# Two row sums ahead of the M sums, one load from another queue, and M_A's blocks in other banks: a gated mix of two linear-attention blocks

## The chip, the core and the metric

One Trainium2 chip; the program runs on one of its cores. The metric is the device time of one execution in microseconds. A run consists of several executions of the changed kernel and of the kernel before on the same chip, and medians are compared. Profiles come from single executions taken with the hardware profiler. In them PE is TensorE (matrix products), PEld its weight loads, DVE is VectorE, ACT ScalarE, POOL GpSimd and SP SyncE; "SPq" and "ACTq" are the instructions with which SyncE and ScalarE start DMA transfers.

## What is computed

The input `x` has 2048 rows of 640 in bf16. Two linear-attention blocks A and B with weights of their own work on the same `x`, and a gate mixes them. Cut to what matters:

```python
g = sigmoid((x * gate_w).sum(-1, keepdims=True))
# for A and for B, with H = 32 heads of Dh = 20:
q, k, v = split(x @ wqkv)
pq, pk = phi(q), phi(k)               # phi(t) = where(t > 0, t + 1, exp(t)) + 1e-6
kv  = einsum("bhsd,bhse->bhde", pk, v)
z   = einsum("bhsd->bhd", pk)
num = einsum("bhqd,bhde->bhqe", pq, kv)
den = einsum("bhqd,bhd->bhq", pq, z)[..., None] + 1e-6
block = (num / den) @ wo
out = g * block_A + (1 - g) * block_B
```

## The kernel before

**The algebra.** The kernel never forms v. For each block it computes G, the product of `x` with `pk` (640 x 640), then kv of each head as the masked blocks of the product of `wv` with G, then M, the product of kv with `wo` (640 x 640). The denominators and the gate go as factors into the rows of `pq` (`scale`, line 760). Then `out` is one product, the row pair of both scaled `pq` times M_A over M_B.

**The stages.** First the k and q products of A with phi behind them (`k_chunk`, `q_block`, `q_strassen`), then G of A, then k and q of B, from about 71 us to 114 us in the profile, in a stage whose PSUM pool is called "weave"; then a stage "after" with G of B, and the M of A in between; then the M of B, and then the output. Many of the products are written as Strassen-Winograd schemes with 7 products for 8, so VectorE makes sums and differences of operands.

**PSUM.** [...] `ps(name, slot)` gives a tile of two banks in one of four numbered slots, a `cell` one bank. "weave" allocates slots 3 and 2 and then four cells `q0` to `q3`, which `q_strassen` calls ce, cf, co and cz. When it closes, slot 2 of the next stage gets a pool of its own ("hold2", on the right side of PSUM, line 1059), and "after" allocates the others on the left as they are first used. A new tile waits for the last users of the tiles whose banks it takes over.

**M_A.** `g_pass` (line 477) makes the last 128 rows of B's G: 16 row blocks of `x`, two products each. In the middle of it, behind 16 of the 32 products, it calls `between` (line 1061), and there the first three of six blocks of M_A are made. `m_a(g, slot)` (line 667) is two products of [120, 120] by [120, 320] into the slot's two banks, a copy by ScalarE to SBUF, and a store of these 120 rows to `m_rows` in DRAM by SyncE (`m_store`, line 664). Blocks 3 and 4 come behind `g_pass` (lines 1062, 1063), block 5 inside `g_strassen` (line 551), always in slot 2. M_A is then read back from DRAM in another layout (row = 5 x partition + index).

**M_B.** Its six blocks (`m_b`, line 675) are made between 139 and 143 us, copied by ScalarE and VectorE half each, and stored by SyncE. Then `m_load` reads M_B back in three loads of two blocks each (rows 0 to 239, 240 to 479, 480 to 639; lines 1097 and 1098). A load waits for the stores of its own rows.

**The output.** The rows of `out` are taken in 8 pairs: pair i is rows 128 i and 1024 + 128 i. With the lower and upper halves of both `pq` as a 2 x 2 block matrix and the column halves of M_A and M_B as another, seven products p1 to p7 of five matmuls each make the four quarters of a pair (class `Pair`, line 784):

- p1 is lower `pq_A` by M_A's left half and p2 lower `pq_B` by M_B's left half; both into bank `w`, which gives quarter c11
- p5 is upper `pq_A` by TM0, into bank `z`
- p6 is the row sum s2 by TM1, on top of p1 in bank `x`; ScalarE copies the result to `u2` (line 837)
- p7 is a row difference (D3) by TM2, into bank `y`; VectorE adds `u2` and gives `u3` (lines 841, 779)
- c22 is the addition of p5 and `u3`; p4, upper `pq_B` by TM3, goes on into bank `y` and p3, the row sum s4 by M_B's right half, on into bank `z`

There are two banks of each kind, for even and odd pairs, so p4 of a pair may begin only when `u3` has read bank `y`.

The operands' sums are VectorE's:

- `p_sums(rows, ks)` (line 722), on 256 rows at a time (two pairs): k=1 adds `pq_B` upper to `pq_A` upper in place, k=2 makes s2 in the lower rows of `xT`, k=4 makes s4 in its upper rows. One is 128 x 1280 elements. `part[0]` serves pairs 0 and 1, `part[1]` pairs 2 and 3, and so on
- `m_sum(k)` (line 733): TM2, TM1 and TM3 from M_B, M_A and TM0, in this order, 128 x 1600 elements each

**The order.** It is written out by hand (lines 1087 to 1148) under a manual schedule: each engine does its instructions in the order in which the program names them, and semaphores are set by the dependences. Around the change it is: blocks 2 to 5 of M_B, with p1 of pair 4 in between; the copy of that p1 to SBUF (`p1_out`, line 1096); the three loads; the scaling of B's last rows (line 1099); `p_sums` with k=1 for parts 0 and 1, k=2 and 4 for part 0; p1 of pairs 5, 6, 7, 2 and 3, then of 0; p5 of pairs 2 and 3; p1 of pair 1; p5 of pairs 0 and 1; the three M sums; `p_sums` with k=2 and 4 for part 1; p2 and c11 of pairs 0 and 1; p7, p6 and c22 of both; p4 and p3 of pair 0; then a loop over pairs 1 to 7.

Of the kernel before, what the change touches and what calls it, by code (L numbers as in the profile page):

```python
# [17 lines left out]
DT = D // P  # L18
# [6 lines left out]
NG = 6  # L25
# [8 lines left out]
def kernel(  # L34
# [11 lines left out]
    nc = tc.nc  # L46
# [12 lines left out]
    def new_stage(name):  # L59

        if stage:
            stage.pop().close()
        if name is not None:
            held = ctx.enter_context(ExitStack())
            stage.append(held)
            pools["ps"] = held.enter_context(late_pool(name))
# [20 lines left out]
    def ps(name, slot=None):  # L87

        return banks(ps_raw(name, slot))
# [387 lines left out]
    def g_pass(b, c, slot, between=None, at=ST // 2):  # L477

        pt = ps(f"g{'AB'[b]}", slot)
        for i in range(ST):  # L480
            if between is not None and i == at:
                between()
            for hf in range(2):
                g_mm(c, i, hf, pt)
        for hf in range(2):
            nc.scalar.copy(out=GT[hf][:, c, :], in_=pt[:, hf, 0:HF])

    def g_mm(c, i, hf, pt):
        nc.tensor.matmul(  # L489
            pt[:, hf, 0:HF], lhsT=xn[:, i, c * P:(c + 1) * P], rhs=pk[:, i, hf * HF:(hf + 1) * HF],  # L490
            start=(i == 0), stop=(i == ST - 1),
        )
# [159 lines left out]
    def m_block(b, g, banks, to=None):  # L652

        at = f_rows[g].start
        for hf in range(2):
            nc.tensor.matmul(
                banks[hf][:K6, 0:HF], lhsT=kv6[b][:K6, at:at + K6], rhs=wo_sb[b][:K6, g, hf * HF:(hf + 1) * HF],
                start=True, stop=True,
            )
        if to is None:  # L660
            to = work.tile([P, D], BF16, tag="osb", name="m5", bufs=3)
        return to[:f_rows[g].stop - at]

    def m_store(g, to):
        nc.sync.dma_start(out=m_rows[f_rows[g], :], in_=to)

    def m_a(g, slot):

        pt = ps("mA", slot)
        to = m_block(0, g, cells(pt), M[0][:, g, :] if g < DT else None)  # L670
        n = to.shape[0]
        nc.scalar.copy(out=to.rearrange("p (b n) -> p b n", b=2), in_=pt[:n, :, 0:HF])
        m_store(g, to)

    def m_b(g, banks):

        to = m_block(1, g, banks, held["mb"][:, g, :] if g < DT else None)
        n = to.shape[0]
        for hf, copy in enumerate((nc.scalar.copy, nc.scalar.copy if g < 2 else nc.vector.tensor_copy)):
            copy(out=to[:, hf * HF:(hf + 1) * HF], in_=banks[hf][:n, 0:HF])  # L680
        m_store(g, to)

    def m_load(g0, g1):

        rows = slice(f_rows[g0].start, f_rows[g1 - 1].stop)
        nc.sync.dma_start(
            out=M[1][rows.start // DT:rows.stop // DT], in_=m_rows[rows, :].rearrange("(p m) d -> p m d", m=DT)
        )

    def cells(pt):  # L690
        return [pt[:, hf] for hf in range(2)]
# [22 lines left out]
    def add_rows(dst, a, b, op):  # L714
        nc.vector.tensor_tensor(out=dst, in0=a, in1=b, op=op)  # L715
# [6 lines left out]
    def p_sums(rows, ks=(1, 2, 4)):  # L722

        up = slice(SH + rows.start, SH + rows.stop)
        a11, a21, a12, a22 = [pqT[b][:, :, r] for b in range(2) for r in (rows, up)]
        s2, s4 = xT[:, :, rows], xT[:, :, up]
        for k, dst, a, b, op in (
            (1, a21, a21, a22, ALU.add), (2, s2, a21, a11, ALU.subtract), (4, s4, a12, s2, ALU.subtract)
        ):
            if k in ks:  # L730
                add_rows(dst, a, b, op)

    def m_sum(k):

        lo, hi = slice(0, HF), slice(HF, D)
        a, b = M[0], M[1]
        if k == 1:
            add_rows(TM[1][:], b[:, :, hi], TM[0][:], ALU.subtract)
        elif k == 2:
            add_rows(TM[2][:], b[:, :, hi], a[:, :, hi], ALU.subtract)  # L740
        else:
            add_rows(TM[3][:], b[:, :, lo], TM[1][:], ALU.subtract)
# [17 lines left out]
    def scale(b, m):  # L760

        rec = R[:].rearrange("p h j n -> p (h j n)")
        nc.vector.tensor_tensor(out=pqT[b][:, m, :], in0=pqT[b][:, m, :], in1=rec, op=ALU.mult)
# [187 lines left out]
    def bank(pool, name, n=1):  # L951
        return pool.tile([P, HB] if n == 1 else [P, n, HB], FP32, tag=name, name=name)

    with tc.manual_schedule():
# [103 lines left out]
        hold = ExitStack()  # L1058
        pools[2] = hold.enter_context(tc.tile_pool(name="hold2", bufs=1, space=bass.MemoryType.PSUM, reuse_waits="tile", side="right"))
        new_stage("after")  # L1060
        g_pass(1, DT - 1, 0, lambda: [m_a(g, slot) for g, slot in enumerate((2, 1, 3))])
        m_a(3, 2)
        m_a(4, 3)
        part = [slice(n * RB, (n + 1) * RB) for n in range(4)]
        held["mb"] = wpool.tile([P, DT, D], BF16, tag="wk", name="MBr")

# [26 lines left out]
        pairs[4].p1(None, (2, 3, 4))  # L1093
        m_b(4, acc["z"])
        m_b(5, acc["w"])
        pairs[4].p1_out()
        for g in range(0, NG, 2):
            m_load(g, g + 2)
        scale(1, 4)
        for rows, ks in ((0, (1,)), (1, (1,)), (0, (2, 4))):  # L1100
            p_sums(part[rows], ks)
# [10 lines left out]
        inner = ctx.enter_context(late_pool("inner"))  # L1112
        acc["y"] = [bank(inner, f"oy{n}") for n in range(2)]
        TM[3] = wpool.tile([P, DT, HF], BF16, tag="wk", name="TM3")
        for k in (2, 1, 3):
            m_sum(k)
        p_sums(part[1], (2, 4))
        for p in pairs[0:2]:
            p.p2()
            p.c11()  # L1120
# [58 lines left out]
```

## Time and profile before

| | us |
|---|---|
| median of 3 runs | 186.67 |
| lowest and highest run | 186.53, 186.91 |
| the profiled execution | 186.59 |
| its span | 184.9 |
| TensorE busy | 179.8 |
| VectorE busy | 148.4 |
| ScalarE busy | 108.5 |

The span runs from the first to the last event of the profiled execution on the core; the device time holds 1.7 us around it. The granted clock of TensorE was 1.0. A row of the timeline gives the start in us, the length in us (of the whole group where it ends in x and a count), the engine, the line of the kernel, the instruction, its output and inputs, and in brackets how long the engine had been idle before it and what released it. [...] In the program's names `xT`, `pqTA`, `pqTB`, `MA`, `MB`, `TM` and `SQ` are SBUF tiles (D3 lies in `SQ`), `ox`, `oy`, `oz`, `ow` the output banks.

### The profile page before, as it was taken

What the parts mean: (1) busy time and instruction counts of PE and PEld (TensorE: products, weight loads), DVE (VectorE), ACT (ScalarE), POOL (GpSimd) and SP (SyncE); (2) the same over time, 40 slices, a digit from 0 to 9 for tenths busy, and PEclk for the clock granted to TensorE, in tenths of its full rate; (3) what the DMA queues carried; (4) which work ended last, traced back from release to release, by engine and by line L of the source; (5) the groups of instructions that cost most, each with busy time, mean ns of one, the idle gap of its engine ahead of it and who ended that gap; (6) DMA issues with size and microseconds to landing.
All of it is one profiled execution on the core that took longest, in us unless ns stands there. A gap on an engine that the chain in (4) does not pass through costs nothing. (4 is left out here: it accounts for less than half of the span.)

```text
span 184.9 us, 3524 instructions
## 1 busy us (share of the span) xinstructions
PE 179.8 (97%) x1357; PEld 120.8 (65%) x1357; DVE 148.4 (80%) x263; ACT 108.5 (59%) x207; POOL 9.1 (5%) x25
## 2 busy tenths in 40 slices
PE   8999999999999999999999999999999998999993
PEld 3666657665667677676666656767678765777772
DVE  0478989999899799898989897969795959678854
ACT  2065489977883553766777778764715745453210
POOL 8920000000000000000000000000000000000000
PEclk9999999999999999999999999999999999999999
DMA  5995559975018000006000000133912830322132
GB/s 181 298 172 78 108 97 330 331 142 177 0 50 230 17 4 0 0 0 181 2 0 0 4 0 2 51 117 117 253 23 63 217 80 0 128 85 76 71 139 74
DMA packets 20848, 18.00 MB, mean 97 GB/s; under 512 B 9120, under 2 KB 20576, under 8 KB 20832
## 3 DMA queue, kind: packets, MB, share of 16 engines
q1 hardware_dynamic: 19968, 16.97, 34.4%
q10 hardware_dynamic: 864, 0.82, 1.3%
q8 instruction: 10, 0.16, 0.4%
q14 instruction: 6, 0.05, 0.1%
HBM read 11.54 MB, written 4.28 MB: 86 GB/s over the span
## 5 line engine op out<-in xcount | busy, mean ns | idle before, releaser
L299 PEld LDWEIGHTS <-xT 128*128 128x128 bf16 x320 | 31.0, 97 | 15.3 <-issue 0.4
L276 DVE TENSOR_SCALAR e<-e 128x640 bf16<-128x640 bf16 (+2 forms) x58 | 19.7, 341 | 6.3 <-ACT e L268 5.9
L299 PE MATMUL kB<-wkB,xT 128*128 128x320 bf16 x160 | 24.2, 299 | 0.0
L299 PE MATMUL kA<-wkA,xT 128*128 128x320 bf16 (+1 forms) x160 | 23.3, 299 | 0.2 <-DMA wkA<-in_A_wqkv_dram 0.2
L268 ACT ACTIVATE e<-q 128x512 bf16<-128x512 f32 x26 | 15.7, 603 | 5.3 <-PE q L417 4.3
L268 ACT ACTIVATE e<-kA 128x640 bf16<-128x640 f32 x16 | 11.3, 713 | 7.7 <-PE kA L299 7.6
L268 ACT ACTIVATE e<-kB 128x640 bf16<-128x640 f32 x16 | 11.4, 710 | 7.6 <-PE kB L299 7.5
L519 PEld LDWEIGHTS <-xn 128*128 128x128 bf16 x128 | 12.3, 98 | 5.4 <-issue 0.6
L352 PE MATMUL qA<-xT,wqA 128*128 128x512 bf16 x60 | 13.4, 379 | 0.0
L352 PEld LDWEIGHTS <-wqA 128*128 128x128 bf16 x64 | 7.5, 118 | 5.9
L287 DVE SCALAR_TENSOR_TENSOR pk<-kB,e 128x640 bf16<-128x640 f32 x12 | 9.9, 822 | 1.0
L837 ACT COPY u<-ox 128x320 f32<-128x320 f32 x8 | 3.4, 426 | 12.4 <-PE ox L774 12.4
L774 PEld LDWEIGHTS <-pqTB 128*128 128x128 bf16 x80 | 7.7, 98 | 4.1 <-issue 1.2
L774 PEld LDWEIGHTS <-xT 128*128 128x128 bf16 x85 | 8.1, 98 | 2.9
L774 PEld LDWEIGHTS <-pqTA 128*128 128x128 bf16 x85 | 8.0, 98 | 2.9
L779 DVE TENSOR_TENSOR osb<-oz,u 128x320 bf16<-128x320 f32 (+1 forms) x18 | 8.0, 453 | 2.3 <-PE oz L774 1.8
L519 PE MATMUL gs<-pk,xn 128*128 128x320 bf16 x64 | 9.4, 299 | 0.0
L287 DVE SCALAR_TENSOR_TENSOR pk<-kA,e 128x640 bf16<-128x640 f32 x10 | 8.2, 820 | 0.9
L435 DVE TENSOR_TENSOR q<-q,p 128x512 f32<-128x512 f32 x12 | 8.3, 692 | 0.8 <-PE q L417 0.6
L268 ACT ACTIVATE e<-qA 128x1024 bf16<-128x1024 f32 x6 | 6.2, 1028 | 4.2 <-PE qA L352 3.9
L489 PEld LDWEIGHTS <-xn 128*128 128x128 bf16 x64 | 6.2, 98 | 3.1 <-issue 0.3
L519 PEld LDWEIGHTS <-S 128*128 128x128 bf16 x64 | 6.0, 98 | 2.6 <-issue 0.5
(193 smaller groups left out, 358.0 us busy)
## 6 DMA issues: line engine op xcount, KB each, us to landing
out_dram<-osb SPq DMA_DIRECT2D x14, 160.0 KB, 1.8
xn<-in_A_x_dram SPq DMA_DIRECT2D x3, 640.0 KB, 5.2
wvA<-in_A_wqkv_dram SPq DMA_DIRECT2D x1, 800.0 KB
wkB<-in_B_wqkv_dram SPq DMA_DIRECT2D x1, 800.0 KB, 4.7
wqB<-in_B_wqkv_dram SPq DMA_DIRECT2D x1, 800.0 KB
wvB<-in_B_wqkv_dram SPq DMA_DIRECT2D x1, 800.0 KB, 4.9
MA<-m_rows SPq DMA_DIRECT2D x1, 800.0 KB
woA<-in_A_wo_dram SPq DMA_DIRECT2D x1, 750.0 KB
```

The lines of the kernel that those rows point to most:

```text
L268: nc.scalar.activation(out=to, in_=part, func=ACT.Exp)
L276: nc.vector.tensor_scalar(self.e, self.e, 1.0, EPS, op0=ALU.min, op1=ALU.add)
L287: nc.vector.scalar_tensor_tensor(out=dst, in0=src, scalar=1.0 + EPS, in1=e, op0=ALU.add, op1=ALU.max)
L299: nc.tensor.matmul(pt[:, hf, 0:n], lhsT=xT[:, c, i * P:(i + 1) * P], rhs=wk[b][:, c, hf * HF:hf * HF + n], start=(c == 0), stop=(c == DT - 1),
L352: nc.tensor.matmul(dst, lhsT=mixed(wq[b][:, c, :], m), rhs=xT[:, c, n * HB:(n + 1) * HB], start=first, stop=last,)
L435: nc.vector.tensor_tensor(out=dst, in0=src, in1=sb, op=ALU.add)
L489: nc.tensor.matmul(pt[:, hf, 0:HF], lhsT=xn[:, i, c * P:(c + 1) * P], rhs=pk[:, i, hf * HF:(hf + 1) * HF], start=(i == 0), stop=(i == ST - 1),
L519: nc.tensor.matmul(pt[:, n, 0:HF], lhsT=left[:, i, n * P:(n + 1) * P], rhs=right[:, i, :], start=(first and i == 0), stop=(i == hc - 1), s ...
L774: nc.tensor.matmul(dst, lhsT=left[:, c, r0:r0 + P], rhs=right[:, c, :], start=(first and c == 0), stop=(c == DT - 1), skip_group_check=not ...
L779: nc.vector.tensor_tensor(out=dst, in0=acc, in1=sb, op=ALU.add)
L837: nc.scalar.copy(out=self.u2[:], in_=self.at("x"))
```

## The change

Four edits in three places:

- `m_load` takes the engine that starts the transfer. The first load, of blocks 0 and 1, is named behind block 5 of M_B and ahead of pair 4's `p1_out`, and ScalarE starts it. The other two stay with SyncE at their place.
- In the stage "after", blocks 0, 1 and 2 of M_A go to slots 1, 3 and 2 (before: 2, 1 and 3).
- Blocks 3 and 4 go to slots 3 and 2 (before: 2 and 3).
- `p_sums(part[1], (2, 4))` stands ahead of the three M sums (before: behind them).

```diff
-    def m_load(g0, g1):
+    def m_load(g0, g1, eng):
 
         rows = slice(f_rows[g0].start, f_rows[g1 - 1].stop)
-        nc.sync.dma_start(
+        eng.dma_start(
             out=M[1][rows.start // DT:rows.stop // DT], in_=m_rows[rows, :].rearrange("(p m) d -> p m d", m=DT)
         )
...
-        g_pass(1, DT - 1, 0, lambda: [m_a(g, slot) for g, slot in enumerate((2, 1, 3))])
-        m_a(3, 2)
-        m_a(4, 3)
+        g_pass(1, DT - 1, 0, lambda: [m_a(g, slot) for g, slot in enumerate((1, 3, 2))])
+        m_a(3, 3)
+        m_a(4, 2)
...
         m_b(5, acc["w"])
+        m_load(0, 2, nc.scalar)
         pairs[4].p1_out()
-        for g in range(0, NG, 2):
-            m_load(g, g + 2)
+        for g in (2, 4):
+            m_load(g, g + 2, nc.sync)
         scale(1, 4)
...
+        p_sums(part[1], (2, 4))
         for k in (2, 1, 3):
             m_sum(k)
-        p_sums(part[1], (2, 4))
         for p in pairs[0:2]:
             p.p2()
```

## The prediction

> **What bounds the kernel now.** I read the page first, then TensorE's waits, the chain of waits, and then the timeline of each engine around the three places that the change touches. The page's first line, and what the waits view answers for TensorE alone from 108 us to the end:
>
> ```profile
> PE 179.8 (97%) x1357; PEld 120.8 (65%) x1357; DVE 148.4 (80%) x263; ACT 108.5 (59%) x207; POOL 9.1 (5%) x25
> PE oy L774 <- DVE u L779: 0.8, 1, 0.8
> ```
>
> TensorE is busy 97% of the span. What can be won without taking work away is therefore its few gaps, and the view names only one for the whole last third: the bank `oy` waited 0.8 us for VectorE's line 779. The chain that ended last, in order of time, shows what stood ahead of that wait:
>
> ```profile
> 153.74 0.74 DVE xT L715
> 154.49 0.02 issue
> 154.51 0.82 DVE xT L715
> ```
>
> Two row sums (`xT`) run right ahead of it. TensorE's timeline at that place (start, length, instruction):
>
> ```profile
> 149.30 1.52 PE L774 MATMUL oz<-TM,pqTA 128*128 128x320 bf16 x10
> 150.78 1.52 PE L774 MATMUL ow<-MB,pqTB 128*128 128x320 bf16 x10
> 152.13 0.84 PE L774 MATMUL oy<-TM,SQ 128*128 128x320 bf16 x5
> 152.81 0.84 PE L774 MATMUL ox<-TM,xT 128*128 128x320 bf16 x5
> 153.49 0.84 PE L774 MATMUL oy<-TM,SQ 128*128 128x320 bf16 x5
> 154.17 0.84 PE L774 MATMUL ox<-TM,xT 128*128 128x320 bf16 x5
> 155.79 0.84 PE L774 MATMUL oy<-TM,pqTB 128*128 128x320 bf16 x5 [0.78 <-DVE u L779]
> ...
> 178.22 0.84 PE L774 MATMUL ox<-TM,xT 128*128 128x320 bf16 x5
> ```
>
> Groups of five products start every 0.68 us (152.13, 152.81, 153.49, 154.17), one product every 0.136. The ten from 149.30, p5 of pairs 0 and 1, would let p2 start at 150.66; it starts at 150.78, **0.12 late**. The five from 154.17, p6 of pair 1, would let p4 of pair 0 start at 154.85; it starts at 155.79, **0.94 late** (the view's 0.78 counts from the modelled end of the last product). From there TensorE sets the pace: the row at 178.22 is 33 groups of five further on, and 22.43 / 33 is 0.68 again. So what is won at 155 us reaches the end in full.
>
> **The row sums.** VectorE's timeline at the same place:
>
> ```profile
> 147.66 0.82 DVE L715 TENSOR_TENSOR xT<-pqTB,xT 128x1280 bf16<-128x1280 bf16 x1
> 150.76 0.99 DVE L715 TENSOR_TENSOR TM<-MB,MA 128x1600 bf16<-128x1600 bf16 x1 [2.27 <-DMA MB<-m_rows]
> 151.67 2.07 DVE L715 TENSOR_TENSOR TM<-MB,TM 128x1600 bf16<-128x1600 bf16 x2
> 153.66 0.82 DVE L715 TENSOR_TENSOR xT<-pqTA 128x1280 bf16<-128x1280 bf16 x1
> 154.51 0.82 DVE L715 TENSOR_TENSOR xT<-pqTB,xT 128x1280 bf16<-128x1280 bf16 x1
> 155.25 0.48 DVE L779 TENSOR_TENSOR u<-oy,u 128x320 f32<-128x320 f32 x1
> ```
>
> Ahead of the first M sum VectorE idles 2.27 us, until B's M has been read back. The two sums that move need 153.66 to 155.33, 1.67 us. Their inputs are ready by then: the k=1 sum of the same rows and the scaling of B's q have run earlier on this engine. Their targets, rows 256 to 511 of `xT` and those 1024 above, are next read for pairs 2 and 3. Put first, they run from 148.50 to 150.17 and end 0.59 before the M sums can begin. They cost nothing; the DMA wait hides them. Only a landing more than 0.59 earlier would take that cover away, and then they would hold up what no product has asked for yet: p7 wants TM2 1.36 after p2 starts.
>
> What is late next at p4? The M sums still end at 153.74. The addition `u` of pair 0 then waits for ScalarE's copy of p6. At the tail the last pair's addition waits for just such a copy, and shows the step between the two engines:
>
> ```profile
> 153.69 0.43 ACT L837 COPY u<-ox 128x320 f32<-128x320 f32 x1 [0.33 <-PE ox L774]
> ```
>
> ```profile
> 179.10 0.43 ACT L837 COPY u<-ox 128x320 f32<-128x320 f32 x1 [2.97 <-PE ox L774]
> ```
>
> ```profile
> 179.56 0.49 DVE L779 TENSOR_TENSOR u<-oy,u 128x320 f32<-128x320 f32 x1 [0.65 <-ACT u L837]
> ```
>
> Start to start that is 0.46, so `u` runs from 154.15 to 154.63. TensorE followed it by 0.06 (155.73 to 155.79), so the bank is free at 154.69; TensorE gets there at 154.85. The slack is 0.16 and the gap closes: **0.94 us**. The addition behind `u` (c22, another 0.5) ends by 155.2, and p3 wants its bank at 155.53.
>
> **M_A's banks.** TensorE around the first M_A blocks, then ScalarE, then VectorE:
>
> ```profile
> 114.68 2.34 PE L489 MATMUL gB<-pk,xn 128*128 128x320 bf16 x16
> 117.08 0.97 PE L656 MATMUL mA<-woA,R 120*120 120x320 bf16 x6
> 117.89 2.34 PE L489 MATMUL gB<-pk,xn 128*128 128x320 bf16 x16
> 120.07 0.71 PE L656 MATMUL mA<-woA,R 120*120 120x320 bf16 x4
> ```
>
> ```profile
> 116.28 0.76 ACT L273 ACTIVATE pqTB<-q,lift 128x512 bf16<-128x512 f32 x1
> 117.55 1.88 ACT L672 CAST MA<-mA 120x640 bf16<-120x640 f32 x3 [0.52 <-PE mA L656]
> ```
>
> ```profile
> 115.81 0.82 DVE L287 SCALAR_TENSOR_TENSOR pk<-kB,e 128x640 bf16<-128x640 f32 x1
> ```
>
> Sixteen products take 2.18 (117.89 to 120.07), so block 0 could start at 116.86. It starts at 117.08, which is 0.04 after ScalarE's activation of `q` ended (117.04). That activation is the last reader of `co` and `cz`, the last two banks that the former stage allocates, and slot 2 belongs to a pool put at the other side of PSUM. With the change block 0 gets slot 1, whose banks were last read by the `kB` chunk (over at 116.63) or, if the layout is another, by something still earlier. Block 0 then starts at 116.86, and block 2, now the one in slot 2, at 117.40, well after 117.04. **0.22 us** come free. What is late next: block 3 needs the copy of block 1, second of the three from 117.55 (0.63 each, so 118.8), block 4 the third (119.43); TensorE comes for them at 120.07. From here to 150 us TensorE's groups and the copies behind them move together. VectorE's sums of k don't, but TensorE's waits view names none that waited for them.
>
> **The first load of B's M.** SyncE's queue, then two rows of the DMA view (the last column is the time from issue to landing), then the issue cost on ScalarE and its timeline:
>
> ```profile
> 141.05 0.98 SPq L665 DMA_DIRECT2D m_rows<-MBr  x2
> 144.77 1.72 SPq L686 DMA_DIRECT2D MB<-m_rows  x3
> 144.77 0.31 SPq L686 DMA_DIRECT2D MB<-m_rows  x1
> ```
>
> ```profile
> m_rows<-MBr SPq DMA_DIRECT2D x5, 150.0 KB, 2.0
> MB<-m_rows SPq DMA_DIRECT2D x1, 200.0 KB, 4.5
> ```
>
> ```profile
> L154 ACTq DMA_DIRECT2D xn<-in_A_x_dram x3: 408/453/454, 0.8 to 2.2; - x3
> 143.62 0.92 ACT L813 COPY GT<-ox 128x320 f32<-128x320 f32 x2
> ```
>
> Load 1 stands at 144.77 behind all six stores on SyncE, though it needs only stores 0 and 1. Store 1 ends its issue at 142.03 and began 0.31 before, at 141.72; 2.0 later, at 143.7, it has landed. ScalarE is through with its copies of M_B at about the same time (the next copy, pair 4's, starts at 143.62), so it hardly waits and issues at about 143.8, 0.97 earlier. Load 3 (the one of 200 KB) goes out at 146.18 (144.77 + 1.72 - 0.31), after the last store's landing, and lands 4.5 later at 150.7. That is the moment that frees VectorE and p2. Is it set by its issue or by the transfers ahead of it? The last two columns here are the share of the DMA engines and GB/s:
>
> ```profile
> 145.50:146.50 1.00, 1.00 (x10) 0.73 (x8) 1.00 (x2) 0.75 (x2) 0.00 (x0) 1.00 0.70 165
> 146.50:149.00 2.50, 2.50 (x20) 1.81 (x19) 1.96 (x3) 1.47 (x5) 0.00 (x0) 1.00 1.04 248
> ```
>
> From 146.5 on they are full, so load 3 waits behind loads 1 and 2; in the microsecond before, 0.30 of their time is free, which an earlier load 1 can fill. So the last landing moves between 0 (the transfers alone decide) and 0.97 (the issue alone decides) earlier, or later if rival 4 holds; I take 0.3, the free share. TensorE can use only the first **0.12** of it, because p5 itself ends at 150.66 behind that.
>
> The cost on ScalarE is one issue of 0.41 to 0.45 and a wait of some 0.1, ahead of pair 4's copy. The banks behind those copies are wanted back late:
>
> ```profile
> 146.58 0.84 PE L774 MATMUL ox<-MA,pqTA 128*128 128x320 bf16 x5
> ```
>
> is p1 of pair 0, which takes pair 4's bank. That copy would now end near 144.7, 1.9 ahead of it, and ScalarE's page share of 59% leaves room to catch up. I cost it at nothing. [...]
>
> [...]
>
> **The sum.** 0.94 + 0.22 + 0.12 - 0.03 = 1.25 us. The profiled execution took 186.59 (its span of 184.9 and 1.7 around it), 0.08 below the median of 186.67 and inside the runs' spread of 186.53 to 186.91. From the median that gives **185.4 us**, 0.7% faster.
>
> **The rivals.**
> 1. The landing doesn't move: the transfers are the limit, as the full engines after 146.5 say, and p2 keeps its 0.12. Then 0.94 + 0.22 = 1.16, so **185.5**. Against it stands the free share before 146.5. [...]
> 2. The bank edit brings nothing, because slot 1 waits as long or slot 2 was not what held block 0. Then 1.03 are left, **185.6**. For it: the waits view names no releaser for these 0.22; I inferred it from two times 0.04 apart. Against it: nothing else ends there.
> 3. Another wait takes p4's place. The slack is 0.16; if `u` of pair 0 came 0.5 later (one more ScalarE copy of 0.43 ahead of it, as ScalarE now has an issue more to do), 0.34 would be lost, **185.75**. Against it: ScalarE waited 0.33 for p6 before that copy.
> 4. Slower: load 1 now shares the engines with stores 2 to 5, and SyncE issues loads 2 and 3 only when these have landed. Each microsecond that the last store lands later goes one to one into load 3, the M sums and p2, and from 1.1 us on it has eaten the rest of the gain. At worst a store beside a load takes as long as a load, 4.5 for 2.0: 2.5 later, less the 1.16, so **188.0**. Against it: the stores of before share the engines among themselves, issued one behind the other, and land in 2.0. For it: they stood ahead of every load in one queue, and now one load is in another.
>
> **How the numbers follow.** Forecast 0.62, rival 1 0.18, rival 2 0.08, rival 3 0.05, rival 4 0.07. A measurement of this kernel can tell about 0.2% (0.37 us) from no change: the runs of before lie 0.14 below to 0.24 above their median. The range takes in the first three cases and rival 3, each with that spread: 185.4 less 0.2 and 185.75 plus 0.2, so 185.2 to 185.95. Of rival 4, 0.03 is a landing late by 0.8 to 1.5, within 0.2%, and 0.04 is later still. So faster 0.93, same 0.03, slower 0.04.
>
> **What would show it.** In the changed kernel VectorE does the two `xT` sums right behind those of part 0, and then still waits some 0.3 us for the load (0.59 less what the landing gains); p4 of pair 0 follows p6 of pair 1 by 0.68, and TensorE's waits view is empty; M_A's block 0 follows the first half of the g pass by 2.18; load 1 stands on ScalarE's queue 0.7 to 1 us ahead of its old place, and p2 follows p5 by 1.36. I am wrong on the load if M lands no earlier, on the banks if block 0 still waits for the end of the activation, and on the whole if p4 keeps a gap or M lands later than 150.7 less 0.22.

## The result and the profile after

| | before | changed |
|---|---|---|
| median of 14 runs each, us | 186.87 | 185.95 |
| lowest and highest, us | 186.44, 187.38 | 185.53, 186.82 |
| profiled execution, us | 186.59 | 186.12 |
| its span, us | 184.9 | 184.4 |

The ratio is 0.9956, with a 95% interval of 0.9943 to 0.9969: 0.44% faster, or 0.82 us of 186.87; the two medians differ by 0.92. The direction was right; forecast were 1.25 us and a range of 185.2 to 185.95, and the median lies at the edge of that. It misses the forecast of 185.4 by 0.55, and 0.20 of this come from the kernel before, which took 186.87 in these 14 runs and 186.67 in the three from which the forecast was counted. The span of the profile fell by only 0.5, because the stage with M_A begins 0.28 us later in it than before, though all the code ahead of it is the same. So the two profiles are compared by distances within a stage.

TensorE around M_A's blocks, and around the output's first pairs, in the changed kernel (start, length):

```profile
114.96 2.34 PE L489 MATMUL gB<-pk,xn 128*128 128x320 bf16 x16
117.13 0.98 PE L656 MATMUL mA<-woA,R 120*120 120x320 bf16 x6
...
149.35 1.52 PE L774 MATMUL oz<-TM,pqTA 128*128 128x320 bf16 x10
151.23 1.52 PE L774 MATMUL ow<-MB,pqTB 128*128 128x320 bf16 x10 [0.36 <-issue]
...
154.63 0.84 PE L774 MATMUL ox<-TM,xT 128*128 128x320 bf16 x5
155.31 0.84 PE L774 MATMUL oy<-TM,pqTB 128*128 128x320 bf16 x5
```

Three distances answer to the three edits. M_A's block 0 follows the g products by 2.17 us (2.40 before): 0.23 won. p4 of pair 0 follows p6 of pair 1 by 0.68 (1.62 before): 0.94 won. But p2 follows p5 by 1.88, where ten products take 1.36 from start to start (1.52 is the row's shown length, 0.16 more): it is 0.52 late, and was 0.12 late before. (The row names no releaser for p2; VectorE's first M sum begins within 0.01 of it, and its row below names the load.) **0.40 us were lost there**, and 0.94 + 0.23 - 0.40 = 0.77 is what the spans show once the later start is taken off (0.5 + 0.28). VectorE at the same place:

```profile
148.46 0.82 DVE L715 TENSOR_TENSOR xT<-pqTA 128x1280 bf16<-128x1280 bf16 x1
149.31 0.82 DVE L715 TENSOR_TENSOR xT<-pqTB,xT 128x1280 bf16<-128x1280 bf16 x1
151.22 0.99 DVE L715 TENSOR_TENSOR TM<-MB,MA 128x1600 bf16<-128x1600 bf16 x1 [1.09 <-DMA MB<-m_rows]
152.13 2.07 DVE L715 TENSOR_TENSOR TM<-MB,TM 128x1600 bf16<-128x1600 bf16 x2
154.61 0.49 DVE L779 TENSOR_TENSOR u<-oy,u 128x320 f32<-128x320 f32 x1 [0.40 <-ACT u L837]
```

The moved row sums ended at 150.13, and VectorE then waited another 1.09 us for the load. So the sums did not push the M sums back; M came late by itself. The loads in the changed kernel: SyncE's queue, what it waited for between 140 and 152 us (in total, times, longest), and ScalarE with its own load. In the queue's rows, one with x2 or x3 spans its whole group, and the row behind it shows the last of the group by itself:

```profile
144.35 0.31 SPq L665 DMA_DIRECT2D m_rows<-m  x1
145.66 3.20 SPq L686 DMA_DIRECT2D MB<-m_rows  x2
148.55 0.31 SPq L686 DMA_DIRECT2D MB<-m_rows  x1
```

```profile
SPq L686 <- DMA m_rows<-m: 1.7, 1, 1.7
SPq L686 <- DMA m_rows<-MBr: 1.6, 2, 0.8
```

```profile
143.90 0.37 ACTq L686 DMA_DIRECT2D MB<-m_rows  x1
144.31 0.76 ACT L813 COPY GT<-ox 128x320 f32<-128x320 f32 x2 [0.54 <-DMA m_rows<-MBr]
144.95 0.44 ACT L813 COPY GT<-mB 128x320 f32<-128x320 f32 x1
```

Load 1 did go out early, at 143.90. Load 3 went out at 148.55, 4.20 behind the last store (144.35), where it was 1.89 before (146.18 and 144.29). The second view says what it stood for last and longest: the landing of that last store, `m_rows<-m`, block 5's 40 rows. Load 3's own time from issue to landing, in the DMA view of the changed kernel, became shorter:

```profile
MB<-m_rows SPq DMA_DIRECT2D x1, 200.0 KB, 2.6
```

2.6 us for 4.5 before, since nothing stood ahead of it any more. The DMA engines show why (last two columns: share, GB/s; first the stretch up to load 3's issue, then the one behind it):

```profile
146.50:148.50 2.00, 2.00 (x17) 1.47 (x15) 1.97 (x4) 1.23 (x4) 0.00 (x0) 1.00 0.80 186
148.50:149.20 0.70, 0.70 (x7) 0.49 (x6) 0.70 (x2) 0.45 (x2) 0.00 (x0) 1.00 0.00 0
149.20:150.40 1.20, 1.20 (x11) 0.88 (x9) 0.90 (x2) 0.51 (x2) 0.00 (x0) 1.00 0.57 171
```

The engines finished loads 1 and 2, whose last packet ended at 148.63. In the 0.7 us of the second row no transfer began, and load 3's first packet came at 149.48. Of the 2.3 us that load 3 went out later, 1.9 came back in its shorter flight, and 0.4 stayed.

### The profile page after: what moved, and what is told of

It is laid out like the page before. It is cut to its first block, busy times and chain, and to the rows that moved or that the text cites. A ratio compares the mean times of both kernels' runs of the same rounds, so it can differ in the third digit from the quotient of the medians.

```text
span 184.4 us, 3525 instructions
## 1 busy us (share of the span) xinstructions
PE 180.2 (98%) x1357; PEld 121.2 (66%) x1357; DVE 148.6 (81%) x263; ACT 108.5 (59%) x207; POOL 9.3 (5%) x25
## 4 chain that ended last, share of the span: by engine, by line
PE 97%; DVE 1%; issue 0%
PE gs L519 17%; PE kA L299 12%; PE kB L299 12%; PE q L417 11%; PE qA L352 7%; PE oy L774 6%; PE oz L774 5%; PE ox L774 4%; PE ow L774 4%; PE q L352 3%; PE gA L489 2%; PE gB L489 2%; PE warm L211 2%; PE qB L352 1%; PE kvA L636 1%; PE xt L254 1%
```

## The experiments

Theory A is: a load that takes up the DMA engines beside M_B's stores makes the last stores land late, and load 3 waits for these. Rival B: the load edit is innocent, and the missing time comes from the other two edits.

### Each edit alone, and the change without the load

```diff
 # no_load: the changed kernel, but with m_load as before (on nc.sync), and
-        m_load(0, 2, nc.scalar)
         pairs[4].p1_out()
-        for g in (2, 4):
-            m_load(g, g + 2, nc.sync)
+        for g in range(0, NG, 2):
+            m_load(g, g + 2)
 # load_only, sums_only, banks_only: the kernel before with that part of the change alone
```

> The changed kernel with all three loads of B's M back on SyncE behind the six stores; row sums and banks stay as changed. Theory A (load 1 on ScalarE's queue makes the last store land late, and load 3 waits for that store): load 3 goes out about 2.0 us after the last store's issue, as in the kernel before, p2 follows p5 of pairs 0 and 1 with 0.12 us lost instead of 0.52, p4 of pair 0 has no gap, and the kernel is 0.94 + 0.23 = 1.17 us faster than before (ratio 0.994), 0.4 us faster than the changed kernel. Rival B (the load is innocent, the missing 0.4 us come from the two other edits, from VectorE's new order for instance): M still lands some 0.4 us late, and the time is that of the changed kernel, 0.8 us below before.

> The kernel before with only the first load of B's M moved to ScalarE. Theory A: load 3 goes out about 148.3 instead of 146.2 and M lands some 0.4 us later; p2, the M sums and p4 move by that, the 0.94 us gap ahead of p4 stays, and the kernel is 0.4 us slower than before (ratio 1.002). Rival B: load 3 goes out at 146.2 and M lands at 150.7 or up to 0.5 earlier: between 0 and 0.12 us faster.

> The kernel before with only the two row sums ahead of the M sums. Theory A: VectorE's 2.27 us of idle time take them in, the M sums start with the landing as before, p4 of pair 0 follows p6 of pair 1 with no gap: 0.94 us faster (ratio 0.995). Rival B: the sums hold the M sums up, and some 0.5 us of that are lost.

> The kernel before with only M_A's blocks in other banks. Theory A: block 0 follows the 16 products ahead of it by 2.18 us instead of 2.40, and everything behind it moves by 0.22: 0.22 us faster (ratio 0.9988), at the limit of what can be measured, so the profile decides. Rival B: block 0 waits as before, or the 0.22 are lost again by 140 us: no change.

| kernel | ratio to before, 95% interval | load 3 behind the last store | p2 late | p4 late |
|---|---|---|---|---|
| before | 1 | 1.89 | 0.12 | 0.94 |
| changed | 0.9956 (0.9943 to 0.9969) | 4.20 | 0.52 | 0 |
| no_load | 0.9928 (0.9904 to 0.9951) | 1.80 | 0 | 0 |
| load_only | 1.0021 (0.9999 to 1.0042) | 4.19 | 0.39 | 0.94 |
| sums_only | 0.9948 (0.9920 to 0.9976) | 1.81 | 0.18 | 0 |
| banks_only | 0.9981 (0.9962 to 1.0001) | 1.88 | 0.39 | 0.94 |

("p2 late" is the distance from p5 of pairs 0 and 1 to p2, less 1.36; "p4 late" that from p6 of pair 1 to p4 of pair 0, less 0.68; times in us.) SyncE's queue without the load edit, and with it alone:

```profile
144.34 0.31 SPq L665 DMA_DIRECT2D m_rows<-m  x1
144.82 1.61 SPq L686 DMA_DIRECT2D MB<-m_rows  x3
146.14 0.30 SPq L686 DMA_DIRECT2D MB<-m_rows  x1
```

```profile
143.63 0.30 SPq L665 DMA_DIRECT2D m_rows<-m  x1
144.91 3.22 SPq L686 DMA_DIRECT2D MB<-m_rows  x2
147.82 0.31 SPq L686 DMA_DIRECT2D MB<-m_rows  x1
```

The 2.3 us between 1.8 and 4.2 come and go with the load edit, whatever the other two do: rival B falls. By the ratios no_load is 1.34 us faster than before, where 1.17 were expected, and load_only 0.39 slower, as expected, though its interval just takes in no change. sums_only came out as expected, 0.97 us by the ratio for 0.94 by the profile. banks_only leaves 2.18 between the g products and block 0, as expected, but in its profile p2 loses 0.27 more behind p5 than before (0.39 for 0.12), so there nothing of the 0.22 reached the end; by its time alone it is not distinguishable from no change. The last landing scatters, too: without the load edit p2 was late by 0 to 0.39 in five profiles (the four here and one below; 0.18 on average), with it by 0.39 to 0.67 in three (0.53). A single profile can't tell the two groups apart, since 0.39 stands in both; by the averages the edit costs some 0.35 us, and the 0.12 which the forecast meant to win is itself within that scatter.

### Which property of load 1 hurts: its time, its queue, its size, its data?

Theory A1 is that load 1 begins ahead of the last store; A2, that it runs in a second queue.

```diff
 # late_scalar, later_scalar: the changed kernel, but load 1 named behind pair 5's (k == 5) or pair 6's (k == 6) product
-        m_load(0, 2, nc.scalar)
...
             pairs[k].p1(to)
+            if k == 5:
+                m_load(0, 2, nc.scalar)
 # early_sync: the changed kernel, but
+        m_load(0, 2, nc.sync)
         m_b(4, acc["z"])
         m_b(5, acc["w"])
-        m_load(0, 2, nc.scalar)
 # half_load: the changed kernel, but
-        m_load(0, 2, nc.scalar)
+        m_load(0, 1, nc.scalar)
         pairs[4].p1_out()
-        for g in (2, 4):
-            m_load(g, g + 2, nc.sync)
+        for lo, hi in ((1, 4), (4, 6)):
+            m_load(lo, hi, nc.sync)
 # other_data: no_load, and ahead of pair 4's p1_out
+        nc.scalar.dma_start(
+            out=xn[0:48, 0:DT, :].rearrange("p c d -> p (c d)"),
+            in_=B_wqkv.rearrange("a b -> (a b)")[0:48 * DT * D].rearrange("(p n) -> p n", p=48),
+        )
```

> The changed kernel with ScalarE's load 1 named behind the first product of pair 5, so that it is issued behind pair 4's and pair 5's copies, at about 144.6 instead of 143.9, and thus behind the last store (144.35). Theory A1 (what hurts is that load 1 begins ahead of the last store): the last store lands within 2.1 us as before, load 3 goes out at 146.3, M lands at about 150.8, the time is that without the load edit, 0.4 us below the changed kernel. Theory A2 (what hurts is a second queue with traffic, whenever it begins): load 3 goes out at 147.5 or later and the time stays within 0.2 us of the changed kernel.

> The changed kernel with load 1 started by SyncE, between stores 3 and 4, at about 143.8, when store 1 has landed: as early as on ScalarE, but in the stores' own queue. Theory A1 (beginning ahead of the last store hurts): the last store lands more than 3 us after its issue and load 3 goes out at 148 or later; time as the changed kernel, or worse since stores 4 and 5 are issued 0.3 later as well. Theory A2 (the second queue hurts): the last store lands 2.0 to 2.6 us after its issue (load 1 ahead of it in one queue), load 3 goes out at 146.6 to 147.2, and M lands at 150.3 to 150.8: 0.3 to 0.4 us below the changed kernel.

> The changed kernel with only block 0 (150 KB instead of 300) loaded by ScalarE, and SyncE's two loads taking blocks 1 to 3 (450 KB) and 4 and 5 (200 KB). Theory A1 or A2 by amount (the store waits for the bytes that the other queue has ahead of it): the last store's delay, some 2 us, halves to about 1; load 3 goes out at about 147.4. Rival (the delay is that of load 2, which stands behind the store in its own queue but shares the engines, so more bytes there make it worse): load 3 goes out at 148.5 or later and M lands as late as in the changed kernel or later.

> The changed kernel with ScalarE's load 1 behind pair 6's copy, issued at about 145.2 us, so 0.85 behind the last store (in the kernel before load 1 was 0.48 behind it, on SyncE). Theory A1 (traffic that begins ahead of the last store hurts): the store lands within 2.1 us and load 3 goes out at 146.3 to 146.6. Theory A2 (traffic in a second queue hurts, even if it begins later): load 3 goes out at 147.5 or later, more than 3 us behind the last store.

> The kernel without the load edit (all three loads on SyncE, row sums and banks as changed), and in the place of ScalarE's load 1 a load of the same size and shape (48 rows of 6400 bytes, 300 KB) of data that nothing uses, from B's weights into a dead part of xn. It adds work and changes no result. Theory A (shared DMA engines: any transfer of that size beside the stores delays them): load 3 goes out 3.5 us or more behind the last store, as in the changed kernel, and M lands later than there, since 300 KB more are moved. Rival C (it matters that the load reads the tensor that the stores write): the last store lands about 2 us after its issue, load 3 goes out at about 146.4, and M lands late by the extra 300 KB alone, some 1.2 us at 248 GB/s.

| kernel | the early load's issue, from the last store's | load 3 behind the last store | p2 late | ratio to before |
|---|---|---|---|---|
| changed | ScalarE, 0.45 ahead | 4.20 | 0.52 | 0.9956 (0.9943 to 0.9969) |
| late_scalar | ScalarE, 0.08 ahead | 4.47 | 0.95 | 0.9968 (0.9952 to 0.9984) |
| later_scalar | ScalarE, 0.54 behind | 1.92 | 0.06 | one run: 185.63 us, before 186.84 |
| early_sync | SyncE, 0.88 ahead | 3.43 | 0.35 | 0.9936 (0.9915 to 0.9956) |
| half_load | ScalarE, 1.03 ahead, 150 KB | 2.91 | 1.69 | 0.9995 (0.9979 to 1.0012) |
| other_data | ScalarE, 1.00 ahead, other data | 3.79 | 1.96 | one run: 187.16 us, before 186.84 |

ScalarE's load and SyncE's queue in late_scalar, then in later_scalar:

```profile
144.50 0.37 ACTq L686 DMA_DIRECT2D MB<-m_rows  x1
```

```profile
144.58 0.31 SPq L665 DMA_DIRECT2D m_rows<-m  x1
145.83 3.53 SPq L686 DMA_DIRECT2D MB<-m_rows  x2
```

```profile
144.86 0.34 ACTq L686 DMA_DIRECT2D MB<-m_rows  x1
```

```profile
144.32 0.31 SPq L665 DMA_DIRECT2D m_rows<-m  x1
145.59 0.96 SPq L686 DMA_DIRECT2D MB<-m_rows  x2
```

In the first the load is issued 0.08 ahead of the last store; load 3 goes out at 149.05 (145.83 + 3.53 - 0.31). In the second it is issued 0.54 behind the store, from the same second queue and beside the same transfers, and load 3 goes out at 146.24, as in the kernel before. late_scalar was meant to be the second of these cases and missed it by 0.1 us; by its number I would have held the queue responsible (A2), and later_scalar refutes that. early_sync agrees from the other side: with load 1 ahead in the stores' own queue the stores are late as well. The rows of SyncE's queue there:

```profile
143.67 0.31 SPq L686 DMA_DIRECT2D MB<-m_rows  x1
144.07 0.37 SPq L665 DMA_DIRECT2D m_rows<-MBr  x1
144.55 0.28 SPq L665 DMA_DIRECT2D m_rows<-m  x1
145.54 2.75 SPq L686 DMA_DIRECT2D MB<-m_rows  x2
```

and what its load 3 waited for, the store of block 4 this time:

```profile
SPq L686 <- DMA m_rows<-MBr: 2.5, 2, 1.9
```

That store needed 3.7 us to land (the longest of its group in the trace), not 2.0. So A1 holds for the stores in these runs: what was issued ahead of them decided. Load 3 went out at 147.98 (145.54 + 2.75 - 0.31), where A1 had said 148 or later. On the time A1 missed: it had said that of the changed kernel or worse, and early_sync is 0.9936 of before, near no_load's 0.9928, with M there at 150.79; A2 had forecast both. So a late load 3 is not yet a late M: its flight was only 2.7 here, and the 0.35 by which p2 is late lies within the scatter of the kernels without the load edit.

other_data answers the question of the tensor. Its extra load, SyncE's queue, and what that waited for:

```profile
143.03 0.38 ACTq L1096 DMA_DIRECT2D xn<-in_B_wqkv_dram  x1
```

```profile
143.12 0.80 SPq L665 DMA_DIRECT2D m_rows<-MBr  x2
144.03 0.28 SPq L665 DMA_DIRECT2D m_rows<-m  x1
144.47 3.66 SPq L686 DMA_DIRECT2D MB<-m_rows  x3
```

```profile
SPq L686 <- DMA m_rows<-MBr: 2.6, 2, 2.4
```

A load of the same size, of weights that the stores have nothing to do with, puts load 3 at 3.79 behind the last store. It is not the reading of `m_rows` that hurts (rival C falls), but 300 KB begun ahead. There the extra load was issued 0.09 ahead of block 3's store (143.03 and 143.12), and load 2 already waited 2.4 for that; the longest landing of its group was 4.2. half_load says that the amount counts: its 150 KB were issued 0.14 ahead of block 3's store (142.95 and 143.09), much like other_data's 300, and the longest landing of the stores' group was 3.2, where it was 4.2 in other_data and 2.1 in the kernel before. Load 3 followed at most 2.9 behind the last store, and right behind load 2 (146.45 and 146.89), so the store itself may have landed sooner. My expectation of 147.4 was 0.5 too late. M landed later than in the changed kernel all the same, as the rival had said, though load 3 was not the reason: 650 KB were still to come when load 2 went out at 146.45.

The traces also keep each DMA packet, and these show when the store's data moved. The stores' packets on SyncE's queue are those of 1280 bytes, one for each of M's 640 rows; the loads' are those of 6400. In the kernel before, the last 40 of the stores' packets, block 5's rows, run from 145.40 to 145.75, ahead of every load's. In the changed kernel they begin only at 146.44, when load 1's have begun (145.21 to 146.46), and end at 147.67, among load 2's, of which the first begins at 146.72. In later_scalar load 3 waited only 0.2 for that store, where it waited 1.7 in the changed kernel. So it is the store's data that came late there, behind the first of the early load's.

### The changed kernel and the one without the load edit side by side

> The changed kernel itself, beside the kernel without the load edit on one chip. Theory A1 (a load that begins ahead of the last store makes it land late): load 3 goes out about 4 us behind the last store, p2 loses about 0.5 us behind p5, as in its first profile; 0.8 us faster than before (ratio 0.9956).

> The kernel with row sums and banks as changed and all three loads on SyncE, a second time, beside the changed kernel. Theory A1: load 3 goes out about 1.9 us behind the last store, p2 loses 0 to 0.2 us, and the kernel is 0.3 to 0.5 us faster than the changed one, 1.1 to 1.3 faster than before (ratio 0.993 to 0.994). Rival: its first result was the luck of one chip, and the two are level.

| kernel | median, us | lowest and highest | ratio to before | load 3 behind the last store | p2 late |
|---|---|---|---|---|---|
| changed | 186.02 | 185.75, 186.30 | 0.9960 (0.9940 to 0.9981) | 4.23 | 0.67 |
| without the load edit | 185.69 | 185.31, 185.77 | 0.9944 (0.9927 to 0.9960) | 1.82 | 0.23 |

SyncE's queue in the changed kernel, then in the one without the load edit:

```profile
144.21 0.30 SPq L665 DMA_DIRECT2D m_rows<-m  x1
145.51 3.24 SPq L686 DMA_DIRECT2D MB<-m_rows  x2
```

```profile
144.31 0.31 SPq L665 DMA_DIRECT2D m_rows<-m  x1
144.79 1.64 SPq L686 DMA_DIRECT2D MB<-m_rows  x3
```

Without the load edit it is 0.33 us faster, and 0.42 when first measured (185.53, against 185.95 then, not on one chip). The intervals of the ratios overlap; of the single runs, the highest of five without the edit (185.77) is just above the lowest of six with it (185.75), and all others stand apart. In the profiles p2 is 0.44 and 0.52 less late. Against before the kernel without the load edit gained 1.05 us by the ratio, a little less than the 1.1 to 1.3 expected, and p2's 0.23 is a little more than the 0 to 0.2. The two edits without the load are the fastest of the three kernels.

## Why the prediction was wrong, point by point

- **What bounds the kernel:** right. TensorE's gaps were the place to look; each of them moved the end by what it lost or won, and the last pair's p6 starts 22.43 behind pair 0's p4 in both kernels (177.74 and 155.31 in the changed one).
- **The row sums, 0.94 us:** right, and to the size. They ran in VectorE's idle time, from 148.46 to 150.13. `u` waited 0.40 for ScalarE's copy, and p4 came with no gap.
- **M_A's banks, 0.22 us:** right in the profile, 0.23 there and 2.17 to 2.18 between the groups in every kernel with this edit. That confirms that slot 2 was what held block 0. That it was the activation which reads `co` and `cz` fits: block 0 starts 0.04 behind its end in the kernel before (117.08 and 117.04), and 0.19 ahead of it in the changed one (117.13 and 117.32).
- **The first load of B's M, 0.12 us won:** this is the step that failed. It put the last landing between 0 and 0.97 earlier, or later only if rival 4 held, and took 0.3 from the engines' free share. The issue of load 1 moved as worked out (143.90 for 143.8), and ScalarE lost nothing by it: its fourth copy behind the load (145.48) was back on its old time (145.42 before, in a profile whose stage with M_A lay 0.05 earlier at block 0). But the landing came 0.46 later on the clock (151.22 for 150.76, the sign of error that the prediction had named for itself), and p2 lost 0.40. A term of +0.12 that measured -0.40 accounts for the whole way from 1.25 to 0.77 but for the 0.03 that the forecast took off for a semaphore more. No run shows that term: in the traces VectorE's first M sum waits for three semaphores in both kernels, and p2 starts within 0.02 of it in both. The step counted load 1's bytes as something that fills free time; it did not ask what stands behind load 1 on the engines and who waits for that. There stood the stores of blocks 4 and 5, which release load 3.
- **Rival 4** had this mechanism and was given 0.07. It named the chain from store to load 3 to p2, and its price of one to one was too high: load 3's flight fell from 4.5 to 2.6, because the transfers ahead of it had drained while it waited, so that 2.3 us of delay cost 0.35 to 0.40. The evidence put up against it (stores sharing the engines among themselves land in 2.0) was no evidence: a store of 150 KB is smaller than a load of 300, and the stores of before had no load ahead of them.
- **The load's engine:** starting load 1 from ScalarE gained nothing here (186.02 with the load edit and 185.69 without it on one chip). What was issued ahead of a store delayed it, from either engine: load 3 went out 4.20 to 4.47 behind the last store with load 1 ahead on ScalarE's queue and 3.43 behind with it ahead on SyncE's, but 1.92 behind with it 0.54 later. By the packets it is the store's data that came late in the changed kernel: block 5's first packet at 146.44, for 145.40 before.

The packets also give most of the size. If the store waited for the early load's bytes alone, 300 KB at the 248 GB/s of the busy stretch would add 1.2 us to its 1.9 (an estimate); it added 2.3 on ScalarE's queue and 1.5 on SyncE's. Of the 2.3, counted from the last store's issue, its first packet began 0.98 later (2.09 for 1.11), and its packets took 0.88 longer (1.23 for 0.35), with load 2's among them. The remaining 0.45 lie between its last packet and load 3's issue (0.88 for 0.43), and their cause stays open. So does why early_sync, with the same order, lost no time.

## What to carry to other kernels

Before a transfer is started earlier, list what is issued right behind it on any queue, and who waits for the landing of that: here the longest landing of the stores' group was 3.2 us with 150 KB begun ahead of block 3's store and 4.2 with 300, for 2.1 in the kernel before, and with the 300 the load behind waited 2.4 for that store. Before work is moved into an engine's idle time, read from the profile when it would end and when the wait that hides it ends: here two row sums in VectorE's idle time ended at 150.13, 1.09 ahead of the end of the wait at 151.22, and cost nothing. When an edit has several parts, measure the kernel without each part: here two parts won 1.17 and the third took a third of it back.

## What the runs showed that I had not expected

- A store of 50 KB let the load behind it go only 4.2 to 4.5 us after its issue when a load of 300 KB had been issued 0.08 to 0.45 us ahead of it, and after 1.9 when that load came 0.54 behind.
- In half_load the last store took 1.36 us of SyncE's time to issue, for some 0.3 otherwise, and ScalarE's load 0.56, for 0.37. The cause stays open:

```profile
143.98 1.36 SPq L665 DMA_DIRECT2D m_rows<-m  x1
```

- The stage with M_A began between 114.00 and 115.19 us in 13 profiles, though all that stands ahead of it is the same in all these kernels. This spread of 1.2 us is larger than the whole change, and no single execution could have shown the result without the distances within the stage.
